# A convolution and a linear attention on one core: the first unit's keys and queries turned by TensorE, in a new instruction order

## The chip, the cores and the metric

The kernel runs on one core of a Trainium2 chip. A core has a matrix engine (TensorE, PE in the profile; its weight loads are listed as PEld), a vector engine (VectorE, DVE), an activation engine (ScalarE, ACT), GpSimd (POOL) and SyncE (SP), which here issues nearly all DMAs. The metric is the device time of one execution in microseconds (us); lower is better. Before the change it was 271.66 us, the median of three runs (271.04 to 272.06).

## The reference

Two layers that share nothing are computed and laid side by side. Layer A works on q, k, v of 2048 positions by 640 channels: a filter of 4 taps over k, a product with v, a long convolution of 2048 taps per channel by FFT, a skip term, and a product with q. Layer B is an attention with 32 heads of 20 channels over 4 segments of 512 positions, with a causal softmax inside a segment and a running memory M, z between segments.

```python
k_shift = sum(k_pad[:, t:t+S, :] * shift_k[:, ks-1-t] for t in range(ks))
kv = k_shift * v
y  = irfft(rfft(kv, 2*S) * rfft(ssm_k, 2*S))[:S] + kv * ssm_D
a  = q * y
# layer B, for each segment s of 512 positions
q, k, v = x @ wq, x @ wk, x @ wv          # split into 32 heads of 20
p   = softmax(q_s @ k_s.T * scale + causal_mask)
o   = g * (phi(q_s) @ M) / (phi(q_s) @ z + 1e-6) + (1 - g) * p @ v_s
M, z = M + phi(k_s).T @ v_s, z + phi(k_s).sum()
b   = o @ wo
out = concatenate([a, b], axis=-1)
```

## The kernel before, in words

Layer A is done in 5 blocks of 128 channels, one call of `conv` each. `load_filter` brings the long filter into the tile `kT`, positions on the partitions: the first block loads it plainly and turns it with 16 matmuls against the identity, and 4 copies out of PSUM write `kT`; the other blocks use a transposing DMA and two more DMAs through memory. `spectrum("K")` multiplies with the DFT table `Wf`; 8 copies from PSUM write the tile `F`, and six vector operations on `F` make `Kh`. `short_filter` brings k in by a transposing DMA into `kr`, applies the taps with matmuls against small diagonal matrices (`skd`, written by ScalarE) and multiplies with v on VectorE into `vt`. `spectrum("X")` makes `Xh` in the way `Kh` is made; `product` multiplies the two spectra on VectorE (its first operation writes `pq` from `Xh` and `Kh`), and `inverse` goes back through the table `Wi`.

Layer B is done in 8 units, a segment and a half of the heads each. `load_x` brings x in; for the first segment four plain loads go into the tile `Y` and TensorE turns them into `xT`. `project` multiplies `xT` with the weights `wqkv`, in groups of five matmuls 320 wide; copies write K and Q side by side into `KQ` and V into `Va`. K and Q of the four blocks of 128 positions are then turned into `KQT` (line 686), in every unit by one transposing DMA per block on SP's queue. After that a bound on the logits is worked out: a chain of VectorE operations in `qabs`, the row maximum `kam`, the small matrix `A`, a matmul, a copy into `qabs`, and four small DMAs that put one row per head group into `KQT`. `attend` then fills tiles `ET` with exponentials: matmuls of `KQT` (ahead of some, the causal mask from the tile `pack`) into PSUM, and two ScalarE activations of 128x1024 per tile. `ET` against `Va` gives the sums, VectorE divides, and `project_out` turns the result and multiplies with `wo`.

A copy from PSUM goes through `evict`, where the string `EVICT` says for each copy in the order of recording whether VectorE (1) or ScalarE (0) does it. All operations are first recorded. Then `issue` (line 256, so all instructions have this line in the profile) emits them in the order that the table `ORDER` gives; `BASE` gives the PSUM bank of each group. Each engine works through its own part of this order without overtaking; a DMA on SP's queue waits, beside its data, for the DMA eight places earlier.

Of the kernel before, what the change touches and what calls it, by code (L numbers as in the profile page):

```python
# [989 lines left out]
ORDER = r"""  # L990
c-jTQ17H{c3<SVW@|kUSwr$&9XWO=I+qOCz?QGk&&ATkf3P(0%M-JpfB;*2+A7v2{xlszyP#Mut0p(B)QBfLIkOyf{0A)}JF%S!R5gFwXfH=s2il~Yx2!(toh~!!cDO3<2hCE8dL`}p-UhRT(S{Oy32t
+Mp)lA5yDK&#uM-6mCDy@S=NR8S^fb5zU^^jg0pc(3-FEXPm3Tu57(dGz^Bxr>;D5~*L0vWYCiXn%#Kr*yOBNWpn$fs?QTYI7*ifcc#L<#MU#^`~P+7wwd9onH6@@s1CgZAivuo#H6nnpXKKZ>H14n=Z
wMkmBYLKM;hIvAz3j1IzR3`0&Gf{{ptFc^Tb7=z&$g|a$LGwBo^hY=W$;uxm0wV;;MZJ4f^bvr8PaNU9OI#yGnfo8;JghMW!fT=nWlduz$F-OPg6g1S5n2xzxRV!*Eor+32Pj_Lwj?fvXrqy+VPQyqIL
JfVam9>`cM->g!QCd@HVmA(;jyBfC+C)cdZQYAmSg6gluI|AiZL0gQM4Raht*7;M4rb~>oJ0#fgxOfC9rP5E;w&cX7@e<M(NSBf+5&B*=P(zMq?4L0)6)pSJoME0I0M=d{L<dqS{Gos_ENXwXrn81A!c
be{jJfghc3cOU5fCw1t+iq6Lpn#*Q02w%P>i!$T4iv)w&!}EV{MVc6t~~5Y-~sAKk2Lw2uzZff`wY(OK7Oc=Xl3dL3PLF}i42izYX5AN_QY4%YMNua|HE>-8cw>Sb)u+X!b@Fhn2XD&kpeTc=TFHEv+2
-oj%%!Wuk599xMnwnv}h0m4aiiEOJ7L*m+c+`(RbhW#2-_UT>3w}W~Q8<4=(B9<kx1G-J0ql2wOfQjwUv)a*KAdbY6xUv!3^(D^fCM32XJ+E6ep2U_U_6l3HpLMdG+TS``YYQ*CHNLz-1RT*_n$%t+x&
2dEB1tUC?2xvxcQ~r2G%=3pTLj2yO<`yBum)=q3DM))My}}zeUFrOQa_-lwX_IwU2o`Rjc73}m0iOpw6fH4MI+fqT-D@qK|dp=rI3{J6)hw^5?Vy*ZeP&LE^2DKq@gU0+|;}J4QcF_-qZUU+HPwqNo$#
{xAm|e$ZARDjy}+T_>PB~#gfS{q?JCFK+;JzODK;tyZyya46t;T#|GMOw3Qr2NpE?ri)FBGme2mcCA|!>u9nd<*-#s1Z7qYev;5XkAbDkwWs(9`&_o7XU&|+jETiO>!lrV`ikL}G3nh7ExMh|Rmdmn8Q
E4YRrLYu~+?HQPS}_YPqbvoATQMmjB`lYWu?|wwidrEVYc;Kal(Ovd-2$z>WtGx4)5cjXt7h$Gmc6tbGTuJe536Cq>h{ViTXC6SVdSGJe_9u*VkKmv^^mGoN+#K4`(<UVla!RM(oK5G6dP@wrJPl;^7h
)EXm=?sQ>~1Il{fa!Dp?<yX8ok1^%Zcom6N&FU&`1gt8I1cv(>dZHr-}eDAu#r+EVJ<GY!oKw$K{cb8T#8rJ=piCf3vzSu=Z~i_O`PVc6W}SvZE}5Sec+?5%#Ym-^lo*gO4eN2NWNTX?o$BYv^+(t#1V  # L1000
!iGvq4v>|$#8z20S#1?$jXl+Y^3@`-lB~7gw#=5Aah<i2KUPs9GXl38d0Yb7jK^fXRhIhPU^{Jx?X~8tDh(Kgy(B94+ddm6(K$jkS~b~Zn{A|=kRXf3+T3DQq_=FfT{c{*%O3lxHRP=gk{EoiyX~DFww
SCf!PZ(rtS!H5U1`T7_Ct@_E3GBRY_J@+nml0Nv=$FqO^L;LJY;d$ij8@~x^s%mkU*&;+iaAaw9|IR&RQFuv(YkE;_`!bVQY?&_-w+d(vjn2lGI^rcI9}PCm(gDbmC-5!1LCWb$QAb$b9L>3)VyuahjZ
!gq$v?Bq@7vp`4eK(o~Z3qW#p)?8)9dCv&8pB;zcZE3>5!FGv6zNn$491Ubz5l7fpQCHt}-8%RGkmc!Ce`tvPQ@f}lhAk*;$(=a`k%1aJlT4vx9SuBH?k$L!@gLzRhF)#CRnLJ}=HkajcNt#I^e&BsRX
JJ0%1LkKDKH>@~z#GiUUR)_dn2p()gSS|amn~R|G7EF^CWrI1tdiR-&RiVEGctn3Sb{_Og{4`BWjT_$xmwEczFd{^tiV#dD{JH_OY)OGkZV$rW4Tt!_(b{2&w5YpSS40w6;|aqe&%?N;t_enb@GkXc*X
8oS-)kkIEJJ7gZFq@Ub8xH%LbXi8m#5F?TTENpPa;*EbQy$i%w*q&tehZD6<(Nb2ynd<c@5Yn=+MiS=4`V9&gDsPT?k*!H@jSivEe4Wjc3AG5^Eswu+VfhCP(kEahvsO&-Zs`Od$b&jnn_MO@6%{*PN^
E#X13j_X;&mvAY?E4%x0uHa5t$;WbsHT|uqKamZ5CQs!qzsoMUXH|S7H*vSTlV=vzpUYKyA@pV3BhT%nY~>HRX5rm@ue_4_{#wHMHtv(ntmkheh}*e?A7u+0_)fl;lKw$<v626j&+<t^`B(WR`=zmekp
uFWVf>r?mI%I^q5YvX@ja~TH|+`kNJM{Rk$f-raX%w_RDWVo`~VN~sa5x;p3?uxAvW{WUcvuLIgjS4yoKMlU`F?t{=#B;Y>(rj&=~%}%6l?T?#=y>#Pt;3(yMwrZ{-IijVJJgp2$txc!0<Ew4T^cQ}wZ
>^J<>n&+sIVFo|dMOrF6{F@#5%#oKvS&*s@Zhf~k8hiCSr-r9S)>oMl^T;A4u`enBF;|#5N`~<Hsly>yIp3fV4ZqM%>yptFAa}1*eyt8-l^9-k5J*-|}3Ge0wy|#zfI^Nr(X?MTKe%{~v_$3bTfj-Im`
c+2IK|a|F`CuR8Q+&0L^N2dshxu?H;n%pv$9q&A;$uCEuJkxM!K3R)ALXljhDX-KI?-qQb;i|MKF8<!XrJeiG>K02`99MZ_*!4*F*K%5^JE%NW9f8X=!-moF7_q9)R*~kkFD!{g>UdZ9$%B{5l^UleWP
#oM7qfXG|2b)Q9tGfeT(n+t$xUl`(Z!e+kJ<h@L=EOJ3YjA`ELIYeKp$N  # L1010
"""
# [76 lines left out]
```

## Time and profile before

| | |
|---|---|
| runs | 271.04, 271.66, 272.06 us |
| profiled execution, its span | 271.3 us |
| PE busy | 259.8 us, 96% |
| ScalarE busy | 249.7 us, 92%, 394 instructions |
| VectorE busy | 246.4 us, 91%, 385 instructions |
| DMA | 44.72 MB, mean 165 GB/s |
| granted TensorE clock | 1.00 |

The profiled execution's time and its span from the first to the last instruction are the same to the tenth, 271.3 us; this lies inside the three runs. Busy time is the union of the instructions of an engine. On PE the instructions are pipelined, so that a busy PE can be one that runs below its pace. Rows of the timeline give the start, the length, the engine, the operation, the tiles (written on the left of the arrow, read on the right), and how often; idle time before an instruction stands in brackets with what ended it. SPq is SP's issuing of DMAs.

### The profile page before, as it was taken

What the parts mean: (1) busy time and instruction counts of PE and PEld (TensorE: products, weight loads), DVE (VectorE), ACT (ScalarE), POOL (GpSimd) and SP (SyncE); (2) the same over time, 40 slices, a digit from 0 to 9 for tenths busy, and PEclk for the clock granted to TensorE, in tenths of its full rate; (3) what the DMA queues carried; (4) which work ended last, traced back from release to release, by engine and by line L of the source; (5) the groups of instructions that cost most, each with busy time, mean ns of one, the idle gap of its engine ahead of it and who ended that gap; (6) DMA issues with size and microseconds to landing.
All of it is one profiled execution on the core that took longest, in us unless ns stands there. A gap on an engine that the chain in (4) does not pass through costs nothing.

```text
span 271.3 us, 10053 instructions
## 1 busy us (share of the span) xinstructions
PE 259.8 (96%) x4335; PEld 194.0 (71%) x4335; DVE 246.4 (91%) x385; ACT 249.7 (92%) x394; POOL 7.2 (3%) x18
## 2 busy tenths in 40 slices
...
GB/s 196 274 217 143 235 178 208 190 243 258 211 164 262 189 153 169 156 183 153 172 219 156 180 148 216 162 170 123 201 165 17 30 159 99 154 89 126 47 51 126
DMA packets 131516, 44.72 MB, mean 165 GB/s; under 512 B 121899, under 2 KB 129072, under 8 KB 131344
## 3 DMA queue, kind: packets, MB, share of 16 engines
...
q8 instruction: 34, 0.56, 0.9%
q0 software_dynamic: 144, 0.12, 0.2%
q14 instruction: 10, 0.08, 0.1%
...
## 4 chain that ended last, share of the span: by engine, by line
PE 66%; ACT 18%; DMA 8%; SPq 3%; issue 2%; DVE 2%; ACTq 0%; DVEq 0%
PE ps L256 66%; ACT ET L256 12%; DMA Wi<-c_wi 3%; SPq L256 3%; ACT F L256 2%; DMA Y<-in_B_x_dram 2%; DMA KQT<-qabs 1%; ACT Va L256 1%; DMA pq<-in_A_q_dram 1%; ACT outb L256 1%; ACT KQ L256 1%; DVE PP L256 1%; ACT PP L256 1%; DVE o L256 0%; DVE outb L256 0%
## 5 line engine op out<-in xcount | busy, mean ns | idle before, releaser
L256 ACT ACTIVATE ET<-ps 128x1024 bf16<-128x1024 f32 x160 | 162.4, 1113 | 0.4 <-PE ps L256 0.4
L256 PE MATMUL ps<-wqkv,xT 128*128 128x320 bf16 x480 | 78.2, 302 | 0.6 <-ACT ET L256 0.3
L256 PEld LDWEIGHTS <-xT 128*128 128x128 bf16 x640 | 58.0, 98 | 28.8 <-issue 7.1
L256 ACT CAST F<-ps 128x512 bf16<-128x512 f32 x72 | 43.9, 683 | 1.3 <-PE ps L256 1.3
L256 PE MATMUL ps<-Va,ET 128*128 128x21 bf16 x1280 | 41.9, 173 | 0.0
L256 PEld LDWEIGHTS <-ET 128*128 128x128 bf16 x1280 | 39.3, 96 | 3.3 <-issue 2.1
L256 PE MATMUL ps<-KQT 32*128 32x128 bf16 (+2 forms) x896 | 34.8, 239 | 0.6 <-DMA KQT<-qabs 0.4
L256 PEld LDWEIGHTS <-Wf 128*128 128x128 bf16 x320 | 29.6, 98 | 6.5 <-issue 1.6
L256 ACT CAST KQ<-ps 128x320 bf16<-128x320 f32 x56 | 26.7, 522 | 1.8 <-PE ps L256 1.8
L256 PE MATMUL ps<-wo,xT 128*128 128x320 bf16 (+2 forms) x160 | 25.5, 299 | 1.3 <-ACT ET L256 1.3
L256 PEld LDWEIGHTS <-KQT 32*128 32x128 bf16 x896 | 16.5, 92 | 10.1 <-issue 7.6
L256 PE MATMUL ps<-kT,Wf 128*128 128x256 bf16 x160 | 22.2, 273 | 0.0
L256 PE MATMUL ps<-vt,Wf 128*128 128x256 bf16 x160 | 21.6, 273 | 0.2
L256 PE MATMUL ps<-Y,Wi 128*128 128x256 bf16 x160 | 20.8, 273 | 0.8 <-DMA Wi<-c_wi 0.8
L256 DVE TENSOR_TENSOR o<-ps,rr 128x640 bf16<-128x640 f32 x24 | 19.7, 820 | 0.4
L256 PE MATMUL ps<-Mbd,PqT 128*128 128x84 bf16 x96 | 18.3, 202 | 1.1 <-ACT ET L256 1.0
L256 DVE TENSOR_TENSOR Y<-Y,pq 128x2048 bf16<-128x2048 bf16 (+1 forms) x20 | 18.6, 943 | 0.0
L256 DVE TENSOR_TENSOR pq<-Xh,Kh 128x2048 bf16<-128x2048 bf16 x15 | 18.3, 1219 | 0.0
L256 ACT CAST Va<-ps 128x320 bf16<-128x320 f32 x31 | 16.0, 536 | 2.2 <-PE ps L256 2.2
L256 PEld LDWEIGHTS <-Wi 128*128 128x128 bf16 x160 | 14.7, 98 | 3.5 <-DMA Wi<-c_wi 1.0
L256 PE MATMUL ps<-skd,kr 128*128 128x128 bf16 (+4 forms) x116 | 16.7, 257 | 0.0
L256 PEld LDWEIGHTS <-kr 128*128 128x128 bf16 x116 | 14.8, 149 | 2.3 <-issue 1.0
...
## 6 DMA issues: line engine op xcount, KB each, us to landing
vt<-in_A_v_dram SPq DMA_DIRECT2D x10, 256.0 KB
pq<-in_A_q_dram SPq DMA_DIRECT2D x10, 256.0 KB
turned<-kT SPq DMA_DIRECT2D x4, 512.0 KB
kT<-turned SPq DMA_DIRECT2D x8, 256.0 KB
out_dram<-pq SPq DMA_DIRECT2D x8, 256.0 KB
out_dram<-outb SPq DMA_DIRECT2D x12, 160.0 KB
kb<-kr SPq DMA_DIRECT2D x6, 256.0 KB
Wf<-c_wf SPq DMA_DIRECT2D x4, 256.0 KB
```

Of the source, the lines that this page charges most:

```text
L256: f(*[fix(a) for a in args], **{k: fix(v) for k, v in kw.items()})
```

## The change

`UTURN = (0,)` sends the first unit's K and Q through the branch that was there unused: for each of the four blocks and for K and Q apart, four matmuls of 128x128 against the identity, into one PSUM bank, and one copy of 128x512 into `KQT`. Four transposing DMAs go, and 32 matmuls and 8 copies come; the new `EVICT` gives 7 of them to ScalarE and 1 to VectorE. `ORDER`, `BASE` and `EVICT` are all new tables, so that the order of all engines moves through the whole program. Nothing else of the code differs.

```diff
-UTURN = ()
+UTURN = (0,)
-EVICT = ("11000000110000001000000010000000...
+EVICT = ("01110011000000110011000000000000...
-ORDER = r"""c-jTQ17H{c3<SVW@|kUSwr$&9XWO=I...
+ORDER = r"""c-jTQ17H{c3<SV@@|kUSwr$&9XWO=I...
-BASE = r"""c-mc30g?nD2qH86|Bo*b+ufU{GBZ...
+BASE = r"""c-lpi2^Pd42t!eV-v7p<pV(=i78F8...
 # in project(u), for each block t of 128 positions
 if u in UTURN:
     for i in range(2):
         g = self.group(1, "kqt")
         with rec.one():
             for k in range(4):
                 nc.tensor.matmul(g.ap[:, 0, 128 * k:128 * k + 128], lhsT=KQ[:, t, i, 4 * k:4 * k + 4, :], rhs=self.ident[:], start=True, stop=True, grp=g)
         self.evict(KQT[:, i, :, tok], g.ap[:, 0, :].rearrange("p (k q) -> p k q", q=128), g)
 else:
     nc.sync.dma_start_transpose(out=KQT[:, :, :, tok].rearrange("p i g t -> p (i g) t"), in_=KQ[:, t])
```

SP's queue from its start, before the change (a number behind a name is the buffer's; `KQT_92` is the first unit's):

```order
L256 DMA wqkv<-in_B_wk_dram 128x5x320
L256 DMA ident<-c_ident 128x128
L256 DMA Y_104<-in_B_x_dram 128x640 x4
L256 DMA kT_105<-in_A_ssm_k_dram 128x2048
L256 DMA wqkv<-in_B_wq_dram 128x5x320
L256 DMA Wf<-c_wf 128x1024 x3
L256 DMA_TRANSPOSE kr<-in_A_k_dram 128x2048
L256 DMA Wf<-c_wf 128x1024
L256 DMA vt_109<-in_A_v_dram 128x8x128 x2
L256 DMA wqkv<-in_B_wv_dram 128x5x320
L256 DMA_TRANSPOSE KQT_92<-KQ 128x8x128 x2
```

The weights of K stand first, the long filter behind x. The same queue from its start, now:

```order
L256 DMA kT_105<-in_A_ssm_k_dram 128x2048
L256 DMA ident<-c_ident 128x128
L256 DMA Wf<-c_wf 128x1024
L256 DMA Y_104<-in_B_x_dram 128x640
L256 DMA Wf<-c_wf 128x1024 x2
L256 DMA Y_104<-in_B_x_dram 128x640
L256 DMA Wf<-c_wf 128x1024
L256 DMA Y_104<-in_B_x_dram 128x640 x2
L256 DMA wqkv<-in_B_wq_dram 128x5x320
L256 DMA wqkv<-in_B_wk_dram 128x5x320
L256 DMA_TRANSPOSE kr<-in_A_k_dram 128x2048
L256 DMA vt_109<-in_A_v_dram 128x8x128 x2
```

The filter and its table have moved to the front, the projection's weights behind x, and the transposes of `KQT_92` are gone. VectorE from its start, before:

```order
L256 MEMSET o_79 128x320
L256 COPY taps<-ps 128x40
L256 CAST xT_102<-ps 128x5x128
L256 TENSOR_SCALAR rr_101<-A_100 128x32
L256 CAST KQ<-ps 128x16x20
L256 TENSOR_SCALAR A_100<-rr_101 128x32
L256 CAST KQ<-ps 128x16x20 x3
L256 CAST kT_106<-ps 128x4x128
L256 CAST F_107<-ps 128x512
L256 TENSOR_SCALAR qabs_74<-KQ 128x1280
L256 TENSOR_TENSOR PP<-PP,qabs_74 128x64x20
```

and now:

```order
L256 MEMSET o_79 128x320
L256 CAST kT_106<-ps 128x4x128
L256 CAST xT_102<-ps 128x5x128
L256 CAST kT_106<-ps 128x4x128
L256 TENSOR_SCALAR A_100<-rr_101 128x32
L256 CAST xT_102<-ps 128x5x128
L256 CAST F_107<-ps 128x512 x2
L256 CAST xT_102<-ps 128x5x128
L256 TENSOR_TENSOR Kh_108<-F_107 128x4x512
L256 TENSOR_TENSOR Kh_108<-Kh_108 128x2x512
L256 TENSOR_TENSOR F_107<-F_107 128x2048
```

The work on the first filter's spectrum (`kT`, `F`, `Kh`) now stands ahead of the copies of K and Q. ScalarE just ahead of its first exponential, before:

```order
L256 CAST F_107<-ps 128x512 x4
L256 CAST Va_91<-rr_101 128x64
L256 CAST Va_90<-ps 128x16x20
L256 CAST qabs_74<-ps 128x512
L256 CAST KQ<-ps 128x16x20
L256 CAST Va_90<-ps 128x16x20
L256 CAST KQ<-ps 128x16x20
L256 ACTIVATE skd_85<-pack,taps 128x64
L256 CAST Va_90<-ps 128x16x20
L256 CAST KQ<-ps 128x16x20 x3
L256 ACTIVATE ET_120<-ps 128x1024 x2
```

and now:

```order
L256 CAST F_107<-ps 128x512 x4
L256 CAST qabs_74<-ps 128x512
L256 CAST KQT_92<-ps 128x4x128 x2
L256 ACTIVATE skd_85<-pack,taps 128x64
L256 CAST KQT_92<-ps 128x4x128
L256 CAST KQ<-ps 128x16x20 x2
L256 CAST KQT_92<-ps 128x4x128
L256 CAST Va_90<-ps 128x16x20
L256 CAST KQ<-ps 128x16x20 x2
L256 ACTIVATE skd_84<-pack,taps 128x64
L256 CAST KQ<-ps 128x16x20
L256 ACTIVATE ET_120<-ps 128x1024 x2
```

Four of the new copies stand between the bound's copy (`qabs`) and the first exponential, and copies of `Va` have moved behind it.

More of the change, by code (lines that the diff above doesn't have):

```diff
@@ L1007 @@
[L1007 to L1010, printed above, removed]
+c-jTQ17H{c3<SV@@|kUSwr$&9XWO=I+qOCz?QGk&&ATj;RkBHT$ssu<m*kc_5>@g_K8YyRL?n_xs!JV-CKaTH<d?cai7pwXrqq(u5?RtnQmH7Fq>VI?f|5*Bnn){YD`h2$n8cOX5-1s@wp5l<QcfC5Q;8vsq_Bh%
@@ new lines @@
+mwHlOT1Yb~B59?x)R)%MMH)+94UlfqT;fP(&8V@YrIeAbQcT)O70IVDC6jcJc+y@HNf@arp(VE_kdBf?lWPIVqnWgm6xCwdS5jy{si3_jtaO+7vRQgcO6?;#wY*l;;#ydHNiHoU;Utxo&>m7mw@H5)AnA3il+{W)
+P%3K`?JT1ugI3j{Qcj1<I2k0>G?fgNF;YW^$w(=!>7=@jkeOOSYU(Jdr9&jGj+fdxNhV5Nogh<Wxu(;}GF_%h8J!^oHMuO(>{>|k>nsh_#kxSJNe(TblXRiB(G{9lCTnVKr|-3`rqPl*TT5vJZKNx8mCn(IT1VIG
+T+J*cWv9&3nbKJIOG0U)d!?vsm!`Tyvg$6GCE2u@&etg#BnM=-G}jh7Rp-cT*(b%Np6-$Q8pX~^OO1qex>lpwVOgRxbgs14lM*5uw3W`6d9pyx$r0J83+1>3OJp3BL$X@eXcF0^izEsn*->e)CuFHE(__*>H|uig
+sGW6-bkfMyMf>O}>8E|Qt9H{w7S_7!Pz|u9(nGh(5;-m5Y`6yLG+ivibc>#mm^NJpX)IeNTQz}g(}XreV_Q_5m%X}Oqhp^A)}9*2c4%mehfC5+`|CvsW4$#F!pi`CEZ1d^4%7>BL$1hWxhqfQo+Pu~x>HB!NR5jz
@@ new lines @@
+`b5U+I32IgWRzZ$U7FlhNPMKU(Yju)$}vr08zcr+%LF~H>1Cp(vYT>3Z^=VhBk}FNq_*4gNTT6^B(<1GYbW)NoYJ*&NS{kOTPLw_T4UH@jg5#F4l5;CZ)$p5CATyIUdTpyDYtcuWw6B9uVd|%B({WzYX|h8X0+E5
+&o)UC>u2E+qDM5m^|vHAs%_BKk|QO~=mm{{v)awx$VJU;?<9@Al}j4I&gnJHWU268Qs9GJ*H3a@Z|G1PWy9>Uw!>)qC|5L#Wwo64NI%O}eWG9Giww5M+Q+h6UyEkZt-IaVwiseP?13i29et=t@lDd=ucXF3&1Mnt
+PhM&O?rIvOLo&S5arRW7>2v)d`R%p7(eF~ge##5|BL!`^6|(X6R(}aG!rtj`DQu1+R>C4k4oi<omK&w4r)9tZD`^95r1i2;$YUub4?-goa#?Q6XBi;?6nU+vWkzZ1ZDlMc%GyLTl(S-%1;wo>CR=&?pi?a`Dp)0}
+Y`IVnRcwk?wP}_g_beZZp*<>EVHCm)D}X`P#H!hMooTbI2%6ast!_(gna#F2mJLm9f_=4y)&X<vn>DiR=!A}FY&lTRx?rBwxA|5a<O1u41~%QkTUR(!NLG}@66=nd7Lj4_!#blBN}!h2ut+R}Pg)waEzm--jxDkt
@@ new lines @@
+_+tw#EW-1%F1EV1+*;tT^+ae!;7@ICEo`N=v}i1cviNN)td;%JaQtUc*$acv+Jw<*?2VW#k9OAHI#?U)Xh#u)ZEY~Zu#<h!SnO<Jxz@gF1+2F&?9JHxs4cP1`mhq>a+P&uMRZ~pTWyuG+16NVZn3S_hC#N?hG4sO
+<_;T*4Yt$baTs=4Tejmy8;(uZ4`6)uM-?2l-IjnosZ7W{7Hr?ND)!nw>&4?1V*Bl+1@MGbLlZV-Gaj(!OvK+h0wZzIs^f?yW*_v$Q9EWotuB69WVXgxOTr6Q1BWaMFIp|MLLAn_dAnri?2lfyKn%bY`>UsHAlfqp
+&)8{8$vPO!0j!OycHLTV6mD2jrs5nN$4#4p(HM(KxMq_v2Dj`OZd(tIM>mecDNIE&Cg%yX;vE~v4xE7rn1=3b$psk1A?(YUScueYg6U|AemqOHG^~fToC~v|tdEQw&RNLJ5j>CC=*W4vfRSu~{>(&LIyS_7xZSl;
+OwSBlgwb4zMtH(39K)w<j4yo4CCJ9H{K~A%&a=qH+|0q83}tzE5_$QK<G2{-FrN9CpUcn;C3q1(`HanR2_-p<6IqJo_?*8u5fykE%kfXoU?o<dJWKO6#R{?zC$S9gTUq|*8%|~c7UmyTWD!naQC4DQ-o_o=#eF<B
```

32 lines of the change are left out of this document (11 added, 21 removed).

## The prediction

> **What bounds the kernel now.** I read the busy shares first, then the busy time by stage, then the timeline of the first 40 us.
>
> ```profile
> PE 259.8 (96%) x4335; PEld 194.0 (71%) x4335; DVE 246.4 (91%) x385; ACT 249.7 (92%) x394; POOL 7.2 (3%) x18
> ```
>
> ```profile
> core 0: us, PE busy (x) PEld busy (x) DVE busy (x) ACT busy (x) POOL busy (x), PEclk, DMA share, GB/s
> 0.00:10.00 10.00, 7.54 (x43) 3.94 (x44) 1.44 (x4) 4.19 (x10) 7.21 (x18) 1.00 0.80 237
> 10.00:30.00 20.00, 19.95 (x162) 15.85 (x161) 14.01 (x25) 14.08 (x35) 0.00 (x0) 1.00 0.92 194
> 30.00:40.00 10.00, 9.63 (x107) 6.39 (x104) 9.65 (x15) 8.83 (x20) 0.00 (x0) 1.00 0.94 196
> 40.00:250.00 210.00, 205.63 (x3719) 155.31 (x3719) 207.39 (x319) 209.28 (x316) 0.00 (x0) 1.00 0.85 166
> 250.00:271.30 21.30, 17.07 (x309) 12.50 (x308) 13.94 (x26) 13.30 (x18) 0.00 (x0) 1.00 0.30 78
> ```
>
> From 40 to 250 us ScalarE stands idle for 0.7 us and VectorE for 2.6. So both are full there, and an operation added to either costs its length. Their idle time lies at the two ends: up to 40 us ScalarE idles 12.9 us and VectorE 14.9, after 250 us 8.0 and 7.4. PE is the busiest by name only, as its own pace shows:
>
> ```profile
> 1.26 2.74 PE L256 MATMUL ps<-o 128*128 128x512 bf16 x6 [1.26 <-DVE o L256]
> 10.10 2.58 PE L256 MATMUL ps<-wqkv,xT 128*128 128x320 bf16 x10
> 13.70 2.26 PE L256 MATMUL ps<-wqkv,xT 128*128 128x320 bf16 x15
> 15.80 0.66 PE L256 MATMUL ps<-ident,kT 128*128 128x128 bf16 x8
> 19.27 1.04 PE L256 MATMUL ps<-kT,Wf 128*128 128x256 bf16 x8
> ```
>
> At 13.70 us a matmul 320 wide takes 0.15 us, at 10.10 it took 0.26; the array is slow at first. At the fast pace a turn of 128 costs 0.08 and a `Wf` product 0.13 (last drain included).
>
> The time is then the moment at which these two engines are full, plus the work that they have left, plus a tail. The tail keeps its make-up: from the 129th `Wi` matmul on, the same 212 matmuls follow in both programs, and of ScalarE's 20 last exponentials and VectorE's last two blocks only a copy or two changes sides. I mark the first moment by ScalarE's first exponential and by VectorE's first product of spectra:
>
> ```profile
> 35.56 0.40 PE L256 MATMUL ps<-pack 32*128 32x128 bf16 x16
> 36.22 1.94 ACT L256 ACTIVATE ET<-ps 128x1024 bf16<-128x1024 f32 x2
> 36.91 1.23 DVE L256 TENSOR_TENSOR pq<-Xh,Kh 128x2048 bf16<-128x2048 bf16 x1
> ```
>
> **The change part by part. Work added.** Prices:
>
> ```profile
> 21.05 2.53 ACT L256 CAST F<-ps 128x512 bf16<-128x512 f32 x5
> 35.18 1.09 ACT L256 CAST KQ<-ps 128x320 bf16<-128x320 f32 x3
> L256 DVE CAST F<-ps 128x512 bf16<-128x512 f32 x8 | 5.5, 687 | 0.7 <-ACT skd L256 0.6
> L256 DVE CAST KQ<-ps 128x320 bf16<-128x320 f32 x8 | 3.8, 489 | 5.3 <-PE ps L256 5.3
> 8.00 0.82 DVE L256 CAST xT<-ps 128x640 bf16<-128x640 f32 x1 [1.72 <-PE ps L256]
> ```
>
> A copy 512 wide costs 0.51 us on ScalarE back to back and 0.69 on VectorE, one 320 wide 0.36 and 0.49. Counted over both orders with the copies that change sides, VectorE gains 4 `F`, 2 `KQ`, 1 `KQT`, 1 `Va`, 1 `kT`, 2 wide `xT` and 1 narrow, and loses 4 `outb` of 320 and two copies of 512: 7 less 2 copies of 512 (3.4), 3 less 4 of 320 (-0.5), 2 of 640 (1.6), less the tap copy, 4.4 in all. ScalarE's 7 `KQT` (3.6) are nearly paid by what it hands over; it ends 0.6 up. What matters is the part behind the marks. Ahead of its first exponential ScalarE has 59 instructions in both programs, now about 0.5 us lighter (`KQT` in, `Va`, `xT`, `kT` out), so 1.1 us more is left behind it. VectorE has 2.3 of its 4.4 ahead of its mark and 2.1 behind.
>
> On PE 32 turns (2.6 at 0.08) come ahead of the first `pack` matmul and 15 projection matmuls (2.3) go behind it. That is even.
>
> **Transposes removed.**
>
> ```profile
> 7.22 6.01 SPq L256 DMA_TRANSPOSE kr<-in_A_k_dram  x1
> 13.90 1.40 SPq L256 DMA_DIRECT2D vt<-in_A_v_dram  x2
> 20.99 2.67 SPq L256 DMA_TRANSPOSE KQT<-KQ  x2
> 24.34 3.30 SPq L256 DMA_TRANSPOSE KQT<-KQ  x2
> ```
>
> SP is freed of 6.0 us. By itself this buys nothing here: while those transposes ran, VectorE was filling the time with `Kh`. It lets the order be another one.
>
> **The start, worked out.** What reaches the core when:
>
> ```profile
> 0.00:5.00 5.00, 3.15 (x8) 0.94 (x8) 0.33 (x1) 1.47 (x2) 3.71 (x11) 1.00 0.56 140
> 5.00:10.00 5.00, 4.40 (x36) 3.00 (x36) 1.11 (x3) 2.71 (x9) 3.50 (x8) 1.00 1.04 333
> 10.00:15.00 5.00, 5.00 (x34) 3.45 (x33) 1.00 (x3) 2.83 (x7) 0.00 (x0) 1.00 1.11 236
> kT<-in_A_ssm_k_dram SPq DMA_DIRECT2D x1, 512.0 KB
> Wf<-c_wf SPq DMA_DIRECT2D x4, 256.0 KB
> Y<-in_B_x_dram SPq DMA_DIRECT2D x4, 160.0 KB
> wqkv<-in_B_wq_dram SPq DMA_DIRECT2D x2, 400.0 KB
> 7.25 1.25 PE L256 MATMUL ps<-ident,Y 128*128 128x128 bf16 x10 [0.36 <-DMA Y<-in_B_x_dram]
> ```
>
> By 5, 10 and 15 us 0.70, 2.37 and 3.55 MB had moved. The second piece of x was byte 0.77 MB of the queue, moved at 5.2 us and usable at 7.25: 2.0 us of lag. The new queue has `kT` at 0.52 MB (usable about 5.5), the last `Wf` at 2.05 with 0.12 MB of small loads (9.0 + 2.0 = 11.0) and the first projection weights at 2.79 (11.8 + 2.0 = 13.8). So the filter's copies start near 6 us, and its last two of eight `F` copies end near 13.3, with the filler matmuls, turns and `Wf` products ahead of them on PE. There `Kh` starts, in place of 23.61:
>
> ```profile
> 23.61 1.23 DVE L256 TENSOR_TENSOR Kh<-F 128x2048 bf16<-128x2048 bf16 x1 [0.68 <-ACT F L256]
> L256 DVE TENSOR_TENSOR Kh<-Kh 128x1024 bf16<-128x1024 bf16 x10 | 6.8, 686 | 0.0
> L256 DVE TENSOR_TENSOR PP<-PP,qabs 128x1280 bf16<-128x1280 bf16 x12 | 9.8, 817 | 0.2
> L256 DVE TENSOR_SCALAR qabs<-KQ 128x1280 bf16<-128x1280 bf16 x12 | 5.8, 483 | 0.0
> ```
>
> From there VectorE's list up to its mark is 4 operations of 2048 (4.9), 8 of 1024 (5.4), 8 of 512 from PSUM (5.5), the sign strip of `KQT` (0.7), 2 `KQ` copies (1.0), the bound's and the memory's SBUF operations (2.6) and three small ones (0.7): 20.8 us, or 34.1. Back to back these overlap by up to 6%, which gives 32.9; waits for v or PE give it back. I take 34.0, a gain of 2.9 (bounds 4.0 and, if v is late, none). With 2.1 more work left, VectorE ends 0.8 earlier.
>
> For ScalarE: the matrix `A` is ready 14.7 us into that list, at 28.0. The bound's matmul (0.4), 25 projection matmuls (3.8), 12 turns (1.0) and the first block (0.66, as from 35.56 to 36.22) follow on PE: 33.9. ScalarE's own list behind the bound (0.5, four `KQT` 2.0, five `KQ` 1.8, small ones 1.1) ends at the same time. The gain is 2.3 (bounds 0.1 and 3.2), against 1.1 more work: 1.2 earlier. As copies lie on either engine, I take the mean of 0.8 and 1.2, so 1.0.
>
> **A stall further on.**
>
> ```profile
> 60.00:80.00 20.00, 18.91 (x331) 14.55 (x329) 19.11 (x31) 19.29 (x29) 0.00 (x0) 1.00 1.06 213
> 59.17 9.11 DMA Wi<-c_wi
> ```
>
> The inverse table, issued at 59.17, came 9.11 us later, and VectorE and ScalarE idled 0.9 and 0.7 in that stretch, half of the 3.3 that they idle together from 40 to 250. In the new queue SP is 6 us ahead, and `Wi` has one DMA fewer ahead of it. Between 0 and 0.7 us is won; I take 0.4.
>
> The sum is 271.3 - 1.0 - 0.4 = 269.9 us of span. The median of the runs lies 0.36 above the profiled span, so 270.2.
>
> **The rivals.** *The array stays slow.* Before, six filler matmuls ran, then PE paused, and the pace was still 0.26 at 10.10; if it holds to 12.2 us again, 6.7 us of PE work from 5.5 on does only half, `Kh` starts near 15.5, and VectorE keeps 0.7 of its gain, ScalarE 0.1: 1.4 and 1.0 later, mean 1.2, less 0.4 for `Wi`, plus 0.36: 272.5, no change by the measure below. For it: the row at 10.10. Against it: ten fillers of 0.43 now run without a pause to 5.5, when `kT` is there. [...]
>
> *V comes late.* SP's transposing load of k held the queue for 6.01 us and the two loads of v came behind it, at 13.90. Now both projection weights stand ahead of it: it is issued near 8.4, the v loads at 14.4 to 15.8. Before, v was used without a wait 7.5 us after its issue; it is needed now after two operations of 2048, three of 1024 and two copies of `KQ`, so at 13.3 + 5.5 = 18.8, 3 us behind the last. If it needs 6, VectorE stops near 21 and its gain is gone: 2.1 us of work on top, 273.4 of span, 273.7 in the median, slower. It decides from the first product of spectra at 35.5 or later. Against it: the second piece of x came in some 5 us with the queue loaded.
>
> *All of it comes.* VectorE at 32.9, ScalarE at 33.0, `Wi` in time: 1.9 and 2.1 earlier, and 0.7 for `Wi`: 269.0 in the median. For it, the full lists at the start; against it, that three waits must all vanish.
>
> **How the numbers follow.** My forecast has 0.50, the slow array 0.26, late v 0.15, all of it 0.09. A difference of 0.5% (1.36 us) is about what a measurement of this kernel can tell from no change: faster is below 270.30, slower above 273.02. The forecast's own range, 268.8 to 271.4, lies on both sides of the first bound: 0.36 of its 0.50 is counted faster. With all of it that is 0.45. Same takes 0.14 of the forecast and 0.21 of the slow array, 0.35; slower has late v and 0.05 of the slow array, 0.20. The range that leaves out 2 in 10 runs from 268.0 to 273.0.
>
> **What would show it.** Right, if `Kh` starts on VectorE by 14, the first product stands near 34 and the first exponential near 33.9; if ScalarE and VectorE then idle under 1 and 3 us up to 250; and if no wait for `Wi` is left. Wrong, if 320-wide matmuls still start 0.26 apart at 10 us, if VectorE waits for v, or if the start is won and PE waits for copies in the long middle, where VectorE now has 2.1 us more.

## The result: 274.4 us, slower by 1.2%

The changed kernel takes 274.38 us (median of four executions, 273.83 to 275.95), the kernel before 271.35 beside it; the ratio is 1.0115, 95% interval 1.0069 to 1.016. Four more executions gave 274.22, ratio 1.015 (1.0082 to 1.0219). The forecast was 270.2, with a range to 273.0.

The start went as forecast, and further. These rows are the timeline of the changed kernel (start, length, engine, operation, tiles, count; in brackets the wait ahead of it):

```profile
5.50 0.88 PE L256 MATMUL ps<-ident,kT 128*128 128x128 bf16 x8
8.11 2.00 PE L256 MATMUL ps<-kT,Wf 128*128 128x256 bf16 x16
13.82 1.22 DVE L256 TENSOR_TENSOR Kh<-F 128x2048 bf16<-128x2048 bf16 x1
18.81 0.68 DVE L256 TENSOR_TENSOR vt<-ps,vt 128x512 bf16<-128x512 f32 x1
26.78 0.28 DVE L256 TENSOR_TENSOR A<-pack,kam 128x128 bf16<-128x128 bf16 x1
32.91 1.23 DVE L256 TENSOR_TENSOR pq<-Xh,Kh 128x2048 bf16<-128x2048 bf16 x1
32.97 2.01 ACT L256 ACTIVATE ET<-ps 128x1024 bf16<-128x1024 f32 x2
```

The array is fast from 8 us on (0.125 us per `Wf` product), `Kh` stands at 13.8, v is there without a wait, the first product of spectra comes 4.0 us earlier than in the profile before and the first exponential 3.25. The busy times of the page and the stages tell where it went. The page of the changed kernel:

```profile
PE 259.2 (95%) x4364; PEld 194.5 (71%) x4367; DVE 249.7 (92%) x390; ACT 251.9 (93%) x397; POOL 7.1 (3%) x18
```

Its three stages, and the worst 20 us among them (busy us of PE, PEld, DVE, ACT, POOL; granted clock, DMA share, GB/s):

```profile
0.00:40.00 40.00, 38.06 (x378) 28.66 (x381) 30.87 (x49) 30.71 (x71) 7.08 (x18) 1.00 0.89 208
40.00:250.00 210.00, 204.09 (x3673) 153.27 (x3670) 205.25 (x318) 206.99 (x310) 0.00 (x0) 1.00 0.85 161
250.00:272.10 22.10, 17.03 (x322) 12.59 (x319) 13.61 (x25) 14.19 (x19) 0.00 (x0) 1.00 0.26 71
100.00:120.00 20.00, 18.71 (x329) 14.43 (x327) 18.04 (x33) 18.32 (x26) 0.00 (x0) 1.00 1.21 172
```

The same stages in a second profile of the kernel before, whose span is 270.5 us:

```profile
0.00:40.00 40.00, 37.31 (x348) 26.72 (x349) 26.24 (x43) 28.07 (x65) 7.22 (x18) 1.00 0.92 212
40.00:250.00 210.00, 205.20 (x3689) 154.82 (x3685) 207.01 (x320) 209.01 (x315) 0.00 (x0) 1.00 0.87 165
250.00:270.50 20.50, 16.44 (x306) 12.13 (x304) 13.16 (x24) 12.50 (x17) 0.00 (x0) 0.98 0.30 77
```

Between 40 and 250 us, where ScalarE and VectorE were full, they now stand idle for 3.0 and 4.75 us (0.7 and 2.6 in the profile before, 1.0 and 3.0 in this second one). The two engines are busy for 251.9 and 249.7 us, 2.2 and 3.3 more than before. Almost half of that idle time lies in one place, 100 to 120 us (3.6 of 7.8 us over both engines). SP's queue there:

```profile
95.60 0.66 SPq L256 DMA_DIRECT2D wo<-in_B_wo_dram  x1
96.31 0.54 SPq L256 DMA_DIRECT2D KQT<-qabs  x1
```

The chain that ended last passes through it:

```profile
96.31 6.04 DMA KQT<-qabs
102.35 1.81 issue
104.16 0.10 DVE qabs L256
```

And so the timeline:

```profile
104.16 0.49 DVE L256 TENSOR_SCALAR qabs<-KQ 128x1280 bf16<-128x1280 bf16 x1 [1.81 <-issue]
105.82 0.59 ACT L256 CAST F<-ps 128x512 bf16<-128x512 f32 x1 [1.61 <-DVE F L256]
107.38 0.81 PE L256 MATMUL ps<-Y,Wi 128*128 128x256 bf16 x6 [1.25 <-ACT ET L256]
```

A 4 KB row of the third unit's bound is issued straight behind the 800 KB of `wo`, and the next operation of VectorE writes into `qabs`, the row's source. It begins 7.85 us after the row's issue. The chain puts 6.04 of these to the row, up to the moment at which VectorE has nothing else left to do, and 1.81 to "issue", a wait for which the profile names no releaser. That it is the row which holds VectorE is so far an inference; `late_own_row` below tests it. VectorE waits 1.8 us, ScalarE behind it 1.6, TensorE behind that 1.25.

The end differs too. ScalarE's last two exponentials, in the second profile before (span 270.5 us) and then in the changed kernel's (272.1):

```profile
257.84 1.94 ACT L256 ACTIVATE ET<-ps 128x1024 bf16<-128x1024 f32 x2 [0.20 <-PE ps L256]
258.96 1.94 ACT L256 ACTIVATE ET<-ps 128x1024 bf16<-128x1024 f32 x2 [0.45 <-PE ps L256]
```

From there to the end it is 12.66 us before and 13.14 now. This holds for all profiles of this study: 12.4 to 12.7 us in the eight that end in the old order, 13.1 to 13.9 in the twelve that end in the new one. In the changed kernel's trace the first part of the last result is copied by 266.3 us, but SP is still issuing stores of `pq` until 267.1 and sends it only then; before, the two moments are 264.9 and 265.0.

**How executions spread.** An execution's time lies 1.7 to 1.9 us above its span in every run (273.83 to 272.1, 272.28 to 270.5), so spans can be compared. Medians and ratios leave out the few executions that lie more than 1.5% above the fastest of the same kernel. Beside medians the table gives the median span of those executions whose mean granted clock (the share of its full clock that TensorE was given) was 0.998 or more: in the profiles of `wo_behind_row`, `own_row_buffer`, `less_scalar` and `join_mended`, all at 0.994 or less, the clock is 0.50 for 3 us and more (the rows of three of them stand below). The kernel before, over 93 executions, has a median of 271.69 us, and 269.9 of span in the 72 with that clock; by the five groups in which it was run beside the others, this span is 269.25 to 270.1, so a few tenths between two runs tell nothing. The changed kernel reached that clock in 3 of 8: 272.1, 272.2 and 272.3 of span. So some 2.3 us lie in the kernel itself.

| run | median us | ratio to before (95%) | span at clock 0.998 or more (executions) |
|---|---|---|---|
| before_again | 271.88 | 0.9995 (0.9967 to 1.0024) | 269.75 (8 of 10) |
| after_again | 274.22 | 1.0150 (1.0082 to 1.0219) | 272.3 (1 of 4) |
| start_new_rest_old | 273.03 | 1.0061 (1.0036 to 1.0086) | 271.05 (8 of 12) |
| start_old_rest_new | 281.05 | 1.0356 (1.0317 to 1.0394) | 279.4 (1 of 4) |
| turn_alone | 278.14 | 1.0262 (1.0220 to 1.0304) | 275.8 (3 of 4) |
| order_alone | 282.06 | 1.0406 (1.0373 to 1.0438) | none of 4 |
| join_mended | 274.13 | 1.0080 (1.0048 to 1.0111) | 270.95 (2 of 6) |
| before_more_scalar | 274.13 | 1.0098 (1.0060 to 1.0136) | 271.7 (3 of 4) |
| wo_behind_row | 273.63 | 1.0067 (1.0046 to 1.0087) | 271.9 (3 of 10) |
| own_row_buffer | 275.00 | 1.0110 (1.0069 to 1.0151) | none of 6 |
| less_scalar | 275.39 | 1.0124 (1.0062 to 1.0186) | 271.4 (1 of 4) |
| gate_fill | 274.27 | 1.0110 (1.0064 to 1.0155) | 272.5 (4 of 4) |
| late_start | 273.75 | 1.0082 (1.0056 to 1.0107) | 271.85 (6 of 7) |
| late_own_row | 273.45 | 1.0055 (1.0025 to 1.0084) | 271.7 (12 of 12) |
| late_less_scalar | 273.41 | 1.0057 (1.0026 to 1.0089) | 271.6 (7 of 12) |
| late_both | 272.67 | 1.0024 (0.9999 to 1.0048) | 270.8 (6 of 12) |
| before_fill | 271.24 | 0.9982 (0.9963 to 1.0002) | 269.4 (10 of 10) |
| before_fill_less | 270.35 | 0.9959 (0.9923 to 0.9995) | 268.6 (11 of 12) |

### The profile page after: what moved, and what is told of

It is laid out like the page before. It is cut to its first block, busy times and chain, and to the rows that moved or that the text cites. A ratio compares the mean times of both kernels' runs of the same rounds, so it can differ in the third digit from the quotient of the medians.

```text
span 272.1 us, 10126 instructions
## 1 busy us (share of the span) xinstructions
PE 259.2 (95%) x4364; PEld 194.5 (71%) x4367; DVE 249.7 (92%) x390; ACT 251.9 (93%) x397; POOL 7.1 (3%) x18
## 4 chain that ended last, share of the span: by engine, by line
PE 66%; ACT 16%; DVE 7%; DMA 4%; issue 4%; SPq 1%; POOL 0%; ACTq 0%; DVEq 0%; POOLq 0%
PE ps L256 66%; ACT ET L256 12%; DMA KQT<-qabs 2%; DVE Y L256 2%; DMA qabs<-in_A_shift_k_dram 2%; DVE pq L256 2%; ACT F L256 1%; SPq L256 1%; DVE Kh L256 1%; DVE F L256 1%; ACT outb L256 1%; ACT PP L256 1%; ACT Va L256 1%; ACT KQ L256 0%; DVE Xh L256 0%
## 5 line engine op out<-in xcount | busy, mean ns | idle before, releaser
L256 PE MATMUL ps<-wqkv,xT 128*128 128x320 bf16 x480 | 76.0, 299 | 0.4 <-ACT KQ L256 0.4
L256 ACT CAST F<-ps 128x512 bf16<-128x512 f32 x68 | 40.2, 662 | 1.9 <-DVE F L256 1.6
L256 PE MATMUL ps<-KQT 32*128 32x128 bf16 (+2 forms) x896 | 34.2, 239 | 0.8 <-ACT ET L256 0.6
L256 PEld LDWEIGHTS <-Wf 128*128 128x128 bf16 x320 | 28.5, 97 | 6.8 <-issue 2.6
L256 ACT CAST KQ<-ps 128x320 bf16<-128x320 f32 x54 | 24.1, 487 | 0.1
L256 PEld LDWEIGHTS <-Wi 128*128 128x128 bf16 x160 | 14.9, 98 | 4.1 <-issue 2.1
L256 ACT ACTIVATE PP<-KQ 128x1280 bf16<-128x1280 bf16 x12 | 15.9, 1335 | 1.3 <-DVE KQ L256 1.3
L256 PE MATMUL ps<-skd,kr 128*128 128x128 bf16 (+4 forms) x114 | 16.0, 255 | 0.1
```

The source lines that it names most:

```text
L256: f(*[fix(a) for a in args], **{k: fix(v) for k, v in kw.items()})
```

## The experiments

**Both kernels once more**, with no edit.

> The kernel before once more, unchanged. The changed kernel's runs lie 1.7 us above their spans (273.83 against 272.1), the run I had of the kernel before lies at its span (271.3). If the profiled execution of before was an ordinary one, this run shows a span near 271.3 and a time near 271.4, and the 3.0 us between the kernels is 0.8 of span and 2.2 outside it. If time outside the span is the same in both, the span here is near 269.7 with 1.7 on top, and the whole 3.0 us lies inside the span.

> The changed kernel once more, unchanged, for more runs and a second trace. If the wait near 104 us belongs to the order (a 4 KB row behind 800 KB of wo on the DMA engines), the second trace has it too: VectorE without work for 1 to 2 us ahead of a qabs operation near 104. If it was an accident of one execution, the second trace has no such gap. The median is expected at 274.4 either way.

The kernel before came out with 270.5 of span and 272.28 us, its other executions at 269.0 to 270.9: what lies outside the span is the same in both kernels, and the profile on which the prediction stood was one of the slower executions. Its start shows why:

```profile
22.48 1.23 DVE L256 TENSOR_TENSOR Kh<-F 128x2048 bf16<-128x2048 bf16 x1 [0.69 <-ACT F L256]
35.08 1.94 ACT L256 ACTIVATE ET<-ps 128x1024 bf16<-128x1024 f32 x2
```

Both rows stand 1.1 us earlier than in the first profile. The changed kernel's second profile began later (`Kh` at 15.31) and has no long gap at 104; its span is 272.6, only 0.5 above the first one's, though its start is 1.5 later. So the gap is not in every execution; of these two it is the one with the early start that has it.

**Which half carries the loss.** The order is cut at the first exponential and the halves of the two kernels are joined.

```diff
 # start_new_rest_old: UTURN = (0,)
-ORDER, EVICT: the changed kernel's
+ORDER, EVICT: the changed kernel's up to the first exponential, then those of before
 # start_old_rest_new: UTURN = ()
+ORDER, EVICT: those of before up to the first exponential, then the changed kernel's
```

> The changed kernel up to its first exponential (turns on TensorE, its order, its choice of copies), then everything else in the order of the kernel before and with its choice of copies. The start theory (the new start is worth its 3.25 us at ScalarE's first exponential and 4.0 at VectorE's first product, and the loss comes from the order and the copies behind it) expects 267 to 269 us. If instead the new start itself leaves work or transfers behind that are paid later, it comes out at 273 to 275, like the changed kernel.

> The kernel before up to its first exponential, then everything else in the order and with the copies of the changed kernel, and no turns on TensorE. The start theory expects the changed kernel's 274.4 plus the lost start, 277 to 278.5 us. If the loss sits in the new start, it comes out near the kernel before, 271 to 272.

The median of the new start with the old rest, 273.03, lies at the lower edge of what the second theory expected (273 to 275). At full clock its span is 271.05, 1.1 under the changed kernel and 1.15 over the one before. That is not a clean halving of the 2.3 us, for the joint has waits of its own:

```profile
33.30 1.09 ACT L256 ACTIVATE ET<-ps 128x1024 bf16<-128x1024 f32 x1
37.50 0.84 PE L256 MATMUL ps<-wqkv,xT 128*128 128x320 bf16 x5 [1.29 <-ACT ET L256]
41.40 0.38 PE L256 MATMUL ps<-pack 32*128 32x128 bf16 x13 [1.10 <-ACT KQ L256]
43.01 0.51 DVE L256 TENSOR_TENSOR Mbd<-ps,pack 128x336 bf16<-128x336 f32 x1 [4.32 <-PE ps L256]
```

ScalarE begins with exponentials at 33.3 us, but the projection that the new order puts off (15 matmuls, 2.2 us) still stands in front of TensorE, its copies in front of ScalarE, and VectorE waits 4.3 us for the first memory product. The old start with the new rest is worse still, 279.4: the new rest is made for a start that has done other work, and there TensorE waits 1.76 us for projection weights that the queue brings later.

**Mending the joint.**

```diff
-copies of KQ, unit 1, blocks 0, 1, 3: ScalarE
+copies of KQ, unit 1, blocks 0, 1, 3: VectorE
-second exponential behind the V copies; memory copy ahead of two operations on spectra
+second exponential ahead of them; memory copy behind them
```

> The new start with the old rest, mended where they join: in that kernel VectorE waited 4.3 us for the first memory product and TensorE 1.3 and 1.1 us for PSUM that ScalarE held. Three KQ copies of unit 1 go from ScalarE to VectorE, one exponential is put ahead of the V copies, and two of VectorE's operations on spectra ahead of the memory copy. If the join was the loss, VectorE and ScalarE lose about 2 us less between them each and the time falls from 273.0 to 270.5 to 271.5. If the turns' copies are the loss, which ScalarE and VectorE pay in full wherever they lie (4.3 us over the two, half of it each, against the same sum of idle time won at the start), it stays at 271 to 272, level with the kernel before, and no lower.

It mended nothing in the median. The KQ copies now stood behind a long operation on VectorE, TensorE waited for them, and its clock fell:

```profile
40.65 0.39 PE L256 MATMUL ps<-pack 32*128 32x128 bf16 x13 [1.70 <-DVE KQ L256]
```

The stages around it:

```profile
38.00:40.00 2.00, 0.90 (x8) 0.44 (x7) 2.00 (x4) 1.14 (x2) 0.00 (x0) 1.00 1.21 267
42.00:44.00 2.00, 1.78 (x18) 1.44 (x17) 0.51 (x1) 1.44 (x2) 0.00 (x0) 0.50 1.15 237
```

Two of its six executions kept the clock: 270.3 and 271.6 of span, no lower than before.

**Is it the turns or the order?** Each alone.

```diff
 # turn_alone, in the order of before: at the place of each transposing DMA
-KQT<-KQ, transposing DMA
+4 matmuls, copy, 4 matmuls, copy
 # order_alone, in the changed order: at the place of a block's last turn
-4 matmuls, copy, 4 matmuls, copy
+KQT<-KQ, transposing DMA
```

> The kernel before in its own order and with its own choice of copies; only the first unit's K and Q are turned by TensorE, at the places where the four transposing DMAs stood (32 matmuls, 8 copies, 7 of them on ScalarE). My prediction had it that freeing SP buys nothing by itself: then the copies fall partly into idle time of the start and the time is 271.5 to 274 (the copies cost 3.6 us on ScalarE and 0.7 on VectorE, of which ScalarE has idle time ahead of its first exponential). The rival, that the transposes were what the start waited for, expects 269 to 271.

> The changed kernel's order and choice of copies, but the first unit's K and Q turned by the four transposing DMAs, each issued where the last turn of its block stood. If the turns are what makes the early start possible, the bound and the first exponential come some 5 us later and the time is 276 to 280. If the order alone makes the start, it is 273 to 275.

Both fell outside what was expected, on the slow side: 278.1 and 282.1. In `turn_alone` ScalarE's `F` copies come late, behind `KQT` copies that wait for their turns, and VectorE waits with `Kh`:

```profile
25.03 1.23 DVE L256 TENSOR_TENSOR Kh<-F 128x2048 bf16<-128x2048 bf16 x1 [4.16 <-ACT F L256]
```

In `order_alone` VectorE waits for the transposing DMAs:

```profile
35.22 0.69 DVE L256 TENSOR_SCALAR qabs<-KQT 128x2048 int16<-128x2048 int16 x1 [7.30 <-DMA KQT<-KQ]
```

Turns and order belong together. "By itself this buys nothing" held; that it costs 7 us by itself (278.14 against 271.02) had not been seen.

**What work costs.** Four copies of the kernel before are done twice; and in the changed kernel four are cut short, to 64 of their 512 columns, so that the rest of `F` keeps what the buffer held.

```diff
 # before_more_scalar, four F copies on ScalarE between 100 and 200 us
 scalar.copy(out, in_)
+scalar.copy(out, in_)
 # less_scalar, four F copies on ScalarE
-self.evict(F[:, c, i], g.ap)
+self.evict(F[:, c, i, 0:64], g.ap[:, :, 0:64])
```

> The kernel before with 4 of ScalarE's F copies of 128x512 done twice, spread from about 100 to 200 us, each straight behind its first. Back to back such a copy takes 0.49 to 0.51 us, 2.0 in all. If ScalarE's work in the middle is paid in full, the time is 2.0 us more than before, 273.5. If there is slack there, it is less than 1 us more.

> The changed kernel with four of ScalarE's F copies between 90 and 150 us cut from 512 columns to 64 (the other columns keep what was in the buffer, so the long convolution of two channel blocks is computed from wrong values): some 1.5 us less on ScalarE. If ScalarE's work is paid in full in the changed kernel too, the time falls by 1.2 to 1.6 us to 272.6 to 273.0. If waits set the pace, it falls by less than 0.7.

In the kernel before, 2.0 us of copies cost 1.8 (271.7 against 269.9 of span): as much as if paid in full, though the three executions spread from 271.3 to 273.0. In the changed kernel the less work gave no less time, but three of four executions had a granted clock of 0.986 to 0.995, and the one that kept its clock stood 0.8 under the changed kernel. This run could not tell.

**The row.** First the neighbours on SP's queue are exchanged, then the rows get a buffer of their own.

```diff
 # wo_behind_row
-wo<-in_B_wo_dram; KQT<-qabs (row 2 of unit 2)
+KQT<-qabs (row 2 of unit 2); wo<-in_B_wo_dram
 # own_row_buffer
-bT = qabs[:, 0]
+bT = self.ring("bT", [128, L])[:]
```

> The changed kernel with two neighbours on SP's queue exchanged: the 800 KB load of wo is issued behind the 4 KB row of unit 2 instead of ahead of it. In the changed kernel that row lands 6.0 us after its issue at 96.31 and VectorE, ScalarE and PE wait 1.8, 1.6 and 1.25 us near 104. If the row waits for wo's packets, the wait goes and the time falls by about 1.8 us, to 272.6. If it waits for the two 256 KB loads of pq ahead of it, or if the time is given back further on, it stays within 0.5 of 274.4.

> The changed kernel in its own order; only the rows of the bound go into a buffer of their own instead of the first rows of qabs, so that VectorE's next operation on qabs doesn't wait until the 4 KB rows have landed. In the changed kernel's trace that wait was 1.8 us at 104 us, and in the trace with the late start there was a second one of 1.5 us at 163. If these waits are what eats the start, the time falls by 1 to 1.8 us, from 274.2 to 272.4 to 273.2, and with them the gap in ScalarE and TensorE behind it. If the time is given back further on, it stays at 273.7 to 274.7.

The exchange brought 0.6 in the median (273.63 against 274.2), 0.3 in span at full clock: between the two expectations, and within what the groups differ by. Its profile has no wait at the row, but its start is 2.3 us late, so the trace doesn't settle it either. `own_row_buffer` was hidden as `less_scalar` was (its six executions have a granted clock of 0.989 to 0.996). By what, `wo_behind_row` shows in its timeline:

```profile
7.25 0.62 PE L256 MATMUL ps<-ident,qabs 5*64 5x5 bf16 x12 [1.08 <-DMA qabs<-in_A_shift_k_dram]
8.84 3.54 PE L256 MATMUL ps<-kT,Wf 128*128 128x256 bf16 x16 [0.24 <-ACT skd L256]
16.13 1.22 DVE L256 TENSOR_TENSOR Kh<-F 128x2048 bf16<-128x2048 bf16 x1
```

and in its stages:

```profile
6.00:7.00 1.00, 0.17 (x3) 0.03 (x1) 0.00 (x0) 1.00 (x2) 1.00 (x2) 1.00 0.79 220
9.00:10.00 1.00, 1.00 (x6) 0.73 (x5) 0.79 (x2) 0.14 (x1) 0.00 (x0) 0.50 1.03 365
```

The same in the timeline of `less_scalar`, after a pause of 1.64 us:

```profile
7.24 0.62 PE L256 MATMUL ps<-ident,qabs 5*64 5x5 bf16 x12 [1.64 <-DMA qabs<-in_A_shift_k_dram]
9.56 3.60 PE L256 MATMUL ps<-kT,Wf 128*128 128x256 bf16 x16
17.34 1.21 DVE L256 TENSOR_TENSOR Kh<-F 128x2048 bf16<-128x2048 bf16 x1
```

In `wo_behind_row` the turns of `kT` were done at 6.2 us, the taps had not come, TensorE paused for 1.1 us, and from 9 to 12 us its granted clock is 0.50: 16 `Wf` products take 3.54 us in place of 2.00, and `Kh` comes 2.3 us later. The length of the pause alone does not decide it: in the profile of `start_new_rest_old` TensorE waits 1.16 us for the taps at the same place, and its clock stays at 1.00; in the first profile of the changed kernel it waits 1.25 us at 107.38, and the clock of the stage from 100 to 120 us is 1.00.

**Keeping the array fast.** Fillers are matmuls whose result nobody reads.

```diff
 # gate_fill: three fillers between the turns of kT and the taps, one ahead of the first Wf products
-WARM, WARMC = 10, 512
+WARM, WARMC = 14, 512
 # late_start: five, all ahead of the first turn of kT
-WARM, WARMC = 10, 512
+WARM, WARMC = 15, 512
```

> The changed kernel with four more filler matmuls on TensorE, three between the turns of kT and the tap matmuls, one ahead of the first Wf products, where TensorE stands idle for 1 to 2 us. In one trace of nearly the same kernel the granted clock fell to 0.50 between 10 and 12 us and 16 Wf products took 3.54 us instead of 2.00. If that pause is what lets the clock fall, the slower half of the executions (275 to 276, mean clock 0.99) goes and the median falls by 0.5 to 1 us, to 273.4 to 273.9. If the clock falls for another reason the median stays at 274.4.

> The changed kernel with five more filler matmuls ahead of the first turn of kT, so that the start is later by 1.0 to 2.1 us (five of 0.21 to 0.43). If what the start wins is carried to the end, the time is 1 to 2 us more than 274.2, 275.2 to 276.3. If it is lost again where the row of unit 2 is awaited near 104 us, the time stays within 0.5 of 274.2.

With either, 10 of 11 executions keep the clock at 0.998 or more, against 3 of 8. But the time hardly falls. In `late_start` the first exponential stands at 33.66, 0.7 later than in the changed kernel's profile, and its span at full clock, 271.85, is not longer than 272.2. Where a lead goes, the operation that writes over the row's source shows. In the first profile of the changed kernel it begins at 104.16 us after a wait of 1.8, in `late_start` (`Kh` at 14.51) at 104.25 after a wait of 0.9. In `gate_fill` (`Kh` at 13.81), and in the second profile of the changed kernel (`Kh` at 15.31):

```profile
104.26 0.49 DVE L256 TENSOR_SCALAR qabs<-KQ 128x1280 bf16<-128x1280 bf16 x1 [1.93 <-issue]
104.23 0.49 DVE L256 TENSOR_SCALAR qabs<-KQ 128x1280 bf16<-128x1280 bf16 x1
```

Starts that lie 1.5 us apart have become the same moment: what was won ahead of it is spent waiting. The profile of `late_start`, taken on its slowest execution, has a second wait of this kind, here with its releaser:

```profile
163.77 0.49 DVE L256 TENSOR_SCALAR qabs<-KQ 128x1280 bf16<-128x1280 bf16 x1 [1.49 <-DMA KQT<-qabs]
```

**Waits and work again, with the array kept fast.** (Of `late_less_scalar` and `late_both` only 7 and 6 of 12 executions reach 0.998; in the profile of the latter, at 0.997, the clock is 1.00 up to 270 us.) The edits of `own_row_buffer`, of eight shortened copies in place of four, and of both, on top of `late_start`.

```diff
 # late_own_row
+bT = self.ring("bT", [128, L])[:]
 # late_less_scalar
+self.evict(F[:, c, i, 0:64], g.ap[:, :, 0:64])   # eight copies
 # late_both: both
```

> The kernel with five more fillers ahead (late_start, 273.75, whose array stays fast in nearly all executions) and the bound's rows in a buffer of their own. In the runs of own_row_buffer and less_scalar the array fell back to half speed in the start (granted clock 0.986 to 0.994, first Kh at 15.3 and 17.3 us instead of 13.8), which hides an effect of 1 us; here it should not. If the waits for the rows (1.8 us at 104, sometimes 1.5 at 163) are paid in the end, the time is 272.2 to 272.9. If not, 273.5 to 274.

> late_start with eight of ScalarE's F copies between 85 and 140 us cut from 512 columns to 64 (two blocks of the long convolution are then computed from values left in the buffer). Each goes from some 0.5 to 0.15 us, 2.8 us of ScalarE's work in all. If ScalarE's work is paid in full, the time is 271.0 to 271.5. If VectorE, which has as much to do (249.8 of busy time against 252.0), takes over as the bound, the gain is 0.5 to 1.5, 272.3 to 273.2. If neither sets the pace, 273.5 to 274.

> Both of the above at once. If row waits and ScalarE's work add up, it gains the sum of the two gains. If the two are the same slack (VectorE's wait for the rows is what leaves ScalarE short of work), it gains no more than the larger one.

By span and median the buffer alone brings 0.15 to 0.3 us and the lighter ScalarE 0.25 to 0.35; together 1.05 to 1.1. By the ratios to the kernel before it is 0.27, 0.25 and 0.58%, which simply add up. Only the gain of both together is clear of the spread, so whether the two depend on each other is not shown. What the single profiles show is where the time lies. With the buffer alone (`Kh` at 14.64) the operation no longer waits:

```profile
103.14 0.48 DVE L256 TENSOR_SCALAR qabs<-KQ 128x1280 bf16<-128x1280 bf16 x1
```

That is 1.0 us ahead of the moment at which it stood in the four profiles with the shared buffer: the row did hold VectorE there. The stage from 100 to 120 us, with the buffer alone:

```profile
100.00:120.00 20.00, 19.96 (x347) 15.58 (x345) 19.70 (x35) 19.82 (x30) 0.00 (x0) 1.00 1.21 174
```

with the lighter ScalarE alone:

```profile
100.00:120.00 20.00, 19.24 (x334) 14.88 (x333) 18.69 (x33) 17.96 (x27) 0.00 (x0) 1.00 1.07 191
```

whose waits have this row (total, times, longest):

```profile
DVE qabs L256 <- issue: 1.3, 1, 1.3
```

and with both:

```profile
100.00:120.00 20.00, 19.95 (x346) 15.55 (x344) 19.69 (x35) 18.83 (x30) 0.00 (x0) 1.00 1.16 198
```

With the buffer alone the wait for the row is gone, but ScalarE has as much to do as ever. With less work on ScalarE alone, the kernel waits for the row again: ScalarE idles 2.0 us there and VectorE 1.3. With both, some of the work that was taken away is won, 1.05 of 2.9 (busy time 252.0 to 249.1); VectorE still has 249.8.

**A version that beats both.** The same remedy on the kernel before.

```diff
 # before_fill: two fillers ahead of the beta product, one behind the taps, one ahead of the first turn of x
+WARM, WARMC = 14, 512
 # before_fill_less: one ahead of the beta product, one behind the taps
+WARM, WARMC = 12, 512
```

> The kernel before with four more fillers where TensorE pauses in its first 8 us (two ahead of the beta product, one behind the taps, one ahead of the first turn of x). In three traces of its start the first Kh operation stood at 21.7, 22.5 and 23.6 us, as the array became fast at some 9, 10 and 12 us. If the pauses set that, the array is fast by 7 us, Kh stands at 21 to 21.7 and the time falls by 0.5 to 1.5 us, to 270 to 271. If not, the fillers cost nothing or up to 0.5 us.

> The kernel before with two more fillers in place of four, one ahead of the beta product and one behind the taps; with four, the beta product came 1.5 us later (6.29) and TensorE waited 0.36 us for ScalarE and 0.64 for VectorE behind it, and the time was 271.24 against 271.69. If the fillers help by an early fast array and the late beta product costs, this is 270.6 to 271.2. If the 0.45 was chance, it is 271.5 to 272.

With two fillers it is 270.35 against 271.54, ratio 0.9959 (0.9923 to 0.9995); with four the gain, 0.45, is not told from nothing. With two, `Kh` stands at 21.45 in the profile. It is the fastest kernel of this study, by little.

## Why the prediction was wrong

It made its sum over the two full engines, so it can be laid beside the traces term by term, as sums of ScalarE and VectorE between the first profile before and the changed kernel, and in the last column between the second profile before and the changed kernel; half of the sum is the span's change.

| term, us over both engines | predicted | measured | from the second profile before |
|---|---|---|---|
| busy time | +5.0 | +5.5 (2.2 and 3.3) | +5.6 |
| idle up to 40 us (gains at the marks, and work moved ahead of them) | -7.0 | -9.4 (12.9 to 9.3, 14.9 to 9.1) | -7.3 |
| idle from 40 to 250 us (`Wi`) | -0.8 | +4.4 (0.7 to 3.0, 2.6 to 4.75) | +3.8 |
| idle after 250 us | 0 | +1.0 | +1.1 |
| half of the sum | -1.4 | +0.8 | +1.6 |

- **Work added.** The sum was right, its shares were not: VectorE +3.3 for 4.4, ScalarE +2.2 for 0.6. The seven `KQT` copies took 4.1 us rather than 3.6: five of them stand alone in the timeline, at 0.58 to 0.62 us, where the back-to-back price of 0.51 had been taken. The rest of ScalarE's excess I can't place in one row. The price itself, work behind the marks in full, agrees with `before_more_scalar`.
- **Transposes removed.** Right in that SP's time buys nothing by itself: `turn_alone` even loses 7 us.
- **The start, worked out.** Right in its steps (`Kh` at 13.3 forecast, 13.8; v without a wait), and the gains came out at their upper bounds, 4.0 and 3.25. But they were measured against an execution of the kernel before that was 1.1 us late itself. Against the second profile before they are 2.9 and 2.1, close to the 2.9 and 2.3 of the forecast, by luck: the marks came 1.1 and 0.9 earlier than forecast, and so did those of the kernel before. "The median of the runs lies 0.36 above the profiled span" was the sign of the late execution and I misread it: in every run since, time lies some 1.77 above a span, so that profile would be of a 273.1 us execution, 1.4 over the median (where the section on time and profile takes its time and span for the same, that too is to be corrected). That is 1.4 of the 4.2 us by which the forecast missed; 2.2 are span, and the rest are executions at a lower granted clock (0.984 to 0.995 in five of eight).
- **A stall further on.** This is the step that failed. It found the one wait of the old middle, for `Wi`, and that wait is indeed gone; from there it took it that a full middle stays full. The new order brings its own waits: 4.4 us of idle time in place of -0.8, 2.6 us of span. The largest is the row's, a DMA that VectorE has to wait for before it may write `qabs` again. I had counted the DMAs of the start by their bytes and none beyond `Wi`.
- **"The tail keeps its make-up."** The make-up, yes, but I put the change of its length at nothing, and it lost 1.0 us of idle time over both engines in the first profile, 0.5 of span, and more in most others of the new order (13.1 to 13.9 us behind the last two exponentials, before 12.4 to 12.7).
- **"The time is then the moment at which these two engines are full, plus the work that they have left, plus a tail."** It holds as an account of an execution, not as a rule for what an edit brings: starting 0.7 us later cost nothing that could be seen, and 2.7 us less work on ScalarE (252.0 to 249.3) brought some 0.3, in a profile in which VectorE again waits at the row.
- **The rivals.** "The array stays slow" came in part: 5 of the 8 executions had a granted clock of 0.984 to 0.995, and in three profiles of the new start at such a clock it did not come by the slow beginning that the rival named but by a pause after it, of 1.08 us in `wo_behind_row`, 1.55 in `own_row_buffer` and 1.64 in `less_scalar`; in the profiles of the new start with such a pause `Kh` stood at 15.3 to 17.3 (15.5 forecast), and the median is 274.2 to 274.4 against some 273.9 to 274.0 (span 272.2 and 1.77) at full clock. Against it stood ten fillers without a pause; that they would make the array fast in time, which the forecast's `Kh` needed too, was an estimate of mine that no run had shown. In the first profile of the changed kernel it was fast (`Wf` products at 0.125 us from 8.11 us on), but it did not stay so in every execution: the clock fell to 0.50 behind these pauses, and behind one of 1.70 us in `join_mended`. "V comes late" did not happen. "All of it comes" did, at the start, and still the kernel is slower.

What stays open: with the rows' wait gone and the array fast the span is 271.7, still 1.8 more than before. The profile of `late_own_row` (272.0), laid beside the second one before (270.5) in the same sum, has +5.7 of busy time, -5.6 of idle time up to 40 us, +0.7 in the middle and +2.2 after 250 us. So there the start just pays for the added work, and most of what is left is the tail. This is a reading of two traces: no run changes the tail alone. The smaller waits don't explain it: TensorE waits 4.1 us for PSUM that ScalarE holds in the first profile of the changed kernel, but 2.9 in the second, as in the second one before.
